# The last store of a gated attention-and-FFN kernel, cut into two halves by partitions and issued from two queues

## The chip, the cores and the metric

The kernel runs on one core of one Trainium2 chip. Its time is device microseconds for one execution: the median of 3 runs is 281.86 us (281.77 to 281.93). One further execution was taken with the hardware profiler; it took 281.68 us.

## What is computed

A sequence of 2048 tokens of width 640 goes through two branches, and a gate per token mixes them. Branch A is linear attention with 32 heads of width 20, whose feature map is a pair of softmaxes. Branch B is an FFN with a gated GELU of width 1728. Cut to what matters:

```python
# x: (1, 2048, 640); all bf16
q, k, v = split_heads(x @ wqkv)
phi(t)  = concat([softmax(t @ w_phi), softmax(-(t @ w_phi))])
kv, z   = einsum("bhsf,bhsd->bhfd", phi(k), v), sum_s phi(k)
a       = (phi(q) @ kv / (phi(q) @ z + 1e-6)) @ wo
b       = (gelu(x @ w_gate) * (x @ w_up)) @ w_down
g       = sigmoid((x * gate_w).sum(-1, keepdims=True))
out     = g * a + (1 - g) * b          # (1, 2048, 640)
```

## The kernel before

All tensors live in on-chip memory. The 2048 tokens are 16 tiles of 128 tokens, in 4 blocks of 4 tiles. Three parts follow one another on TensorE: the projections and the attention state (`attention_state`), the up and gate products of the FFN (`gateups` in `ffn`), and the products with `w_down` and `wo`, which close the kernel (`downs`, line 999).

`downs` calls `down_pair` (line 912) for two token tiles at a time. Its matmuls sum, in PSUM, the FFN half (`wd_sb`) and the attention half (`wo_sb`) of one piece of the output; each sum is made of two halves of the array's rows, so a piece of the output has an opening pass and a closing one (lines 963 to 978). When a piece is closed, `evac` (line 940) moves it from PSUM to the tile `outsb`, multiplied by the gate of each token `Gm`: ScalarE with an activation (line 948), or, for the last pair of tiles, ScalarE for one column piece and VectorE for the other (line 946).

For the last pair of tiles (`last`) the pieces are cut finer, so that less is left to do after the last matmul (lines 917 to 919): tile 14 in one store of 640 columns, tile 15 in one of 448 (two pieces of 224) and a last one of 192 (two pieces of 96). Each of these three stores is one DMA of 128 partitions from `outsb` to the output in HBM, issued by SyncE (lines 953 and 954). The last of them, 128 rows of 192 bf16 numbers, is 48 KB, 384 bytes to the row.

The order of all work is written out by hand. A small recording layer, `_Sched`, turns each operation into an instruction on its engine and adds the semaphore waits that its reads and writes need. `op` (line 66) is for compute instructions. `dma` (line 84) is for transfers. Each queue has a number of lanes, one semaphore to a lane, taken in turn: 16 for SyncE's queue (`sp`), 4 for ScalarE's (`act`), 2 for GpSimd's (line 144). A transfer waits, on the engine that issues it, until the last transfer on its lane has landed, and until what it reads is written. ScalarE's queue carries two small loads at the start of the kernel (lines 276 and 279), and nothing after that.

At the end `finish` (line 99) makes SyncE wait for every engine's semaphore and then for the last transfer of each lane of each queue, in the order in which they were issued. These waits close the program: its last instruction is SyncE's wait for the last store.

Of the kernel before, what the change touches and what calls it, by code (L numbers as in the profile page):

```python
# [3 lines left out]
P = 128  # L4
# [103 lines left out]
class _Kernel:  # L108
# [803 lines left out]
    def down_pair(self, t0, banks, last):  # L912

        sc = self.sc
        NFC, KD, D = self.NFC - 1, self.KD, self.D
        hk = t0 // 4
        if last:
            parts = [((t0, 0, 320), (t0, 320, 320)), ((t0 + 1, 0, 224), (t0 + 1, 224, 224)),
                     ((t0 + 1, 448, 96), (t0 + 1, 544, 96))]
        else:  # L920
            parts = [((t0, c, 320), (t0 + 1, c, 320)) for c in (0, 320)]
        nw = len(parts)

        def mm(r, j, h, c, opens, x, n):
            t, w0, w = parts[h][j]
            tt, gs, bk, a = t % 4, t % 8, banks[h][j], 64 * r
            end = x == n - 1
            if c <= NFC:
                lhs, rhs = self.hT(hk, c)[a:a + 64, tt * P:(tt + 1) * P], self.wd_sb[a:a + 64, c, w0:w0 + w]
                rd = [("hT", hk, c), "wd"] if c < NFC else [("hT", hk, 13, r), ("wd13", r)]  # L930
            else:
                k = c - NFC - 1
                lhs, rhs = self.goT[a:a + 64, gs, k, :], self.wo_sb[a:a + 64, k, w0:w0 + w]
                rd = [("goT", gs), "wo"]
            sc.op("pe", lambda e: e.matmul(self.bank(bk, w), lhs, rhs, start=opens and x == 0, stop=end and not opens,  # L935
                                           skip_group_check=True),
                  reads=rd, writes=[("ps", bk)] + ([("turn", bk)] if end else []), signal=end,
                  after=[("turn", bk)] if x == 0 and not opens else ())

        def evac(h):  # L940
            for j in (0, 1):
                t, w0, w = parts[h][j]
                bk, dst, g = banks[h][j], self.outsb[:, t % 4, w0:w0 + w], self.Gm[:, t:t + 1]
                rd, wr = [("ps", bk), "Gm"], [("outsb", t % 4, h, j)]
                if last and j == 1:
                    sc.op("dve", lambda e: e.tensor_scalar(dst, self.bank(bk, w), g, None, op0=ALU.mult), reads=rd, writes=wr)
                else:
                    sc.op("act", lambda e: e.activation(dst, self.bank(bk, w), AF.Copy, scale=g), reads=rd, writes=wr)  # L948
            os_ = t0 % 4
            if last:  # L950
                c1 = w0 + w
                c0 = parts[h][0][1]
                sc.dma("sp", lambda e: e.dma_start(self.out[t * P:(t + 1) * P, c0:c1], self.outsb[:, t % 4, c0:c1]),
                       reads=[("outsb", t % 4, h, j) for j in (0, 1)], writes=[("out", t0, h)])
            elif h == nw - 1:
                if t0 < self.TB:
                    rows = self.out[0:self.BT, :].rearrange("(p j) n -> p j n", j=self.TB)[:, t0:t0 + 2, :]
                else:
                    rows = self.out[t0 * P:(t0 + 2) * P, :].rearrange("(j p) n -> p j n", p=P)
                sc.dma("sp", lambda e: e.dma_start(rows[:, :, :], self.outsb[:, os_:os_ + 2, :]),  # L960
                       reads=[("outsb", os_ + j, k, j) for j in (0, 1) for k in range(nw)], writes=[("out", t0, h)])

        wos = [NFC + 1 + k for k in range(KD)]
        opening = list(range(NFC + 1)) + wos
        for part in (range(NFC + 1), range(NFC + 1, len(opening))):
            for h in range(nw):
                for x in part:
                    for r in (0, 1):
                        mm(r, r, h, opening[x], True, x, len(opening))
                    yield None  # L970
        closing = list(range(NFC)) + wos
        for h in range(nw):
            for x, c in enumerate(closing):
                for r in (0, 1):
                    mm(r, 1 - r, h, c, False, x, len(closing))
                if c == closing[-1]:
                    evac(h)
                yield None
# [104 lines left out]
```

## Time and profile before

| what | value |
|---|---|
| median of 3 runs | 281.86 us (281.77 to 281.93) |
| the profiled execution: its time | 281.68 us |
| its span, first to last instruction | 280.4 us |
| around the span | 1.28 us |
| granted TensorE clock | 1.000 |
| TensorE matmul busy | 276.6 us (99%) |
| VectorE busy | 177.3 us (63%) |
| ScalarE busy | 106.4 us (38%) |
| DMA rate, mean over the span | 86 GB/s |
| transfers on SyncE's queue (q1) | 59296 packets, 23.63 MB |
| transfers on ScalarE's queue (q10) | 666 packets, 0.03 MB |

The span is counted from the first instruction to the end of the last one; the time of an execution has some more around it. "Busy" is the time in which an engine has an instruction in work. The instructions that issue DMAs, and those that wait for semaphores, are not counted as busy. A DMA has an issue, a time on the engine that sends it off, and a landing, when its semaphore is complete; between the two, its packets run on the core's 16 DMA engines, which all queues share.

### The profile page before, as it was taken

To read this page: it belongs to the slowest core of one execution; us is meant where nothing else is said; L and a number is where in the kernel's file an instruction comes from. 1 tells how busy PE (TensorE), PEld (TensorE's weight loads), DVE (VectorE), ACT (ScalarE), POOL (GpSimd) and SP (SyncE) were. 2 spreads that over 40 slices of the span, in tenths; PEclk is the share of its full clock that TensorE was granted. 3 is DMA by queue.
4 is the path that set the end of the run, shared out by engine and by line. 5 is a ranking of instruction groups with operands and counts; after the bars stand their busy time and mean duration, and the time that the engine had idled before them with its cause. 6 is when DMAs were issued, how large, how long until landed. Compare 5 with 4: busy or idle time off the path is not lost.

```text
span 280.4 us, 7063 instructions
## 1 busy us (share of the span) xinstructions
PE 276.6 (99%) x2994; PEld 168.1 (60%) x3006; DVE 177.3 (63%) x342; ACT 106.4 (38%) x205; POOL 14.4 (5%) x69
## 2 busy tenths in 40 slices
PE   8999999999999999999999999999999999999997
PEld 4576766666765444444444444445777777777785
DVE  2666999999998524233242234878884883883801
ACT  3347877878783423222323223122112112112021
POOL 7411001101000000000000000000000000000000
DMA  7999069887899910000000000101133142232221
GB/s 217 224 220 189 6 136 165 171 163 146 162 191 273 347 41 0 2 0 0 1 2 0 0 0 2 23 2 26 26 50 108 35 76 56 62 59 66 71 75 47
DMA packets 59994, 24.11 MB, mean 86 GB/s; under 512 B 50874, under 2 KB 59450, under 8 KB 59962
## 3 DMA queue, kind: packets, MB, share of 16 engines
q1 hardware_dynamic: 59296, 23.63, 37.7%
q8 instruction: 23, 0.38, 0.6%
q10 hardware_dynamic: 666, 0.03, 0.2%
q14 instruction: 9, 0.07, 0.1%
HBM read 9.04 MB, written 2.62 MB: 42 GB/s over the span
## 4 chain that ended last, share of the span: by engine, by line
PE 97%; DMA 1%; issue 0%; SPq 0%; ACT 0%
PE ps L466 52%; PE ps L935 29%; PE ps L832 6%; PE ps L610 4%; PE ps L480 2%; PE ps L875 2%; PE ps L646 2%; DMA xtok<-in_A_x_dram 1%; PE ps L406 1%; PE ps L342 0%; SPq L230 0%; ACT outsb L948 0%; PE ps L371 0%
## 5 line engine op out<-in xcount | busy, mean ns | idle before, releaser
L809 ACT ACTIVATE gl<-ps 128x512 bf16<-128x512 f32 x52 | 31.1, 597 | 71.2 <-PE ps L466 56.3
L466 PE MATMUL ps<-xT,wu_sb 128*128 128x512 bf16 x214 | 52.9, 379 | 0.3
L466 PE MATMUL ps<-xT,wg_sb 128*128 128x512 bf16 x214 | 52.7, 379 | 0.3
L466 PE MATMUL ps<-w,xT 128*128 128x368 bf16 (+6 forms) x340 | 51.6, 303 | 0.0
L813 DVE TENSOR_TENSOR hT<-ps,gl 128x512 bf16<-128x512 f32 x34 | 23.4, 691 | 44.5 <-PE ps L466 44.5
L935 PE MATMUL ps<-wd_sb,hT 64*128 64x320 bf16 x648 | 48.2, 296 | 0.0
L948 ACT ACTIVATE outsb<-ps,Gm 128x320 bf16<-128x320 f32 (+2 forms) x31 | 14.6, 516 | 70.3 <-PE ps L935 70.3
L466 PEld LDWEIGHTS ps<-w,xT 128*128 128x128 bf16 x340 | 32.1, 98 | 14.6
L935 PEld LDWEIGHTS ps<-wd_sb,hT 64*128 64x128 bf16 x648 | 30.9, 94 | 11.8
L466 PEld LDWEIGHTS ps<-xT,wu_sb 128*128 128x128 bf16 x220 | 21.5, 98 | 25.6
L466 PEld LDWEIGHTS ps<-xT,wg_sb 128*128 128x128 bf16 x220 | 21.2, 98 | 25.2 <-issue 0.2
L935 PE MATMUL ps<-wo_sb,goT 64*128 64x320 bf16 (+2 forms) x340 | 26.5, 288 | 0.0
L628 DVE TENSOR_REDUCE Dk<-Ek 128x66 f32<-128x1320 bf16 x16 | 24.3, 1520 | 2.3 <-ACT gcol L539 2.3
L637 DVE TENSOR_TENSOR Ek<-Ek,Dk 128x1320 bf16<-128x1320 bf16 x16 | 24.5, 1533 | 0.5
L904 DVE TENSOR_TENSOR O<-ps,RH 128x640 bf16<-128x640 f32 x32 | 24.8, 815 | 0.0
L549 ACT ACTIVATE Ek<-ps 128x627 bf16<-128x627 f32 x32 | 20.5, 693 | 6.0 <-PE ps L610 4.5
L549 ACT ACTIVATE Eqt<-ps 128x627 bf16<-128x627 f32 x32 | 20.6, 704 | 2.4 <-PE ps L466 2.4
L935 PEld LDWEIGHTS ps<-wo_sb,goT 64*128 64x128 bf16 x340 | 15.8, 94 | 5.5
L832 PE MATMUL ps<-xT,wg_sb 64*128 64x512 bf16 x80 | 17.6, 376 | 0.0
L832 PE MATMUL ps<-xT,wu_sb 64*128 64x512 bf16 x80 | 17.6, 376 | 0.0
L935 PE MATMUL ps<-wd_sb,xT 64*128 64x320 bf16 (+2 forms) x270 | 16.0, 269 | 0.0
L893 DVE RECIPROCAL RH<-ps 128x32 f32<-128x32 f32 x16 | 5.7, 356 | 13.4 <-PE ps L875 13.4
(97 smaller groups left out, 222.3 us busy)
## 6 DMA issues: line engine op xcount, KB each, us to landing
out_dram<-outsb SPq DMA_DIRECT2D x7, 320.0 KB, 2.9
wd_sb<-in_B_w_down_dram SPq DMA_DIRECT2D x1, 2080.0 KB, 12.2
wg_sb<-in_B_w_gate_dram SPq DMA_DIRECT2D x5, 224.0 KB, 3.1
wg_sb<-in_B_w_gate_dram SPq DMA_DIRECT2D x5, 192.0 KB, 3.0
wu_sb<-in_B_w_up_dram SPq DMA_DIRECT2D x5, 192.0 KB, 3.9
wo_sb<-in_A_wo_dram SPq DMA_DIRECT2D x1, 800.0 KB, 10.2
xtok<-in_A_x_dram SPq DMA_DIRECT2D x2, 320.0 KB, 3.2
w<-in_A_wqkv_dram SPq DMA_DIRECT2D x4, 160.0 KB, 3.6
```

The lines of the kernel that those rows point to most:

```text
L466: self.sc.op("pe", lambda e: e.matmul(self.ps[:, bank * 512 + c0:bank * 512 + c0 + n], lhs, rhs, start=first, stop=fin), reads=reads, writ ...
L549: self.sc.op("act", lambda e: e.activation(dst, src, AF.Exp, scale=scale), reads=[("ps", b), ("ps", b + 1)], writes=[(name, sl, s)])
L610: self.sc.op("pe", lambda e: e.matmul(out, self.xT[:, kt, t * P:(t + 1) * P], self.w3[:, kt, c:c + 2 * n].rearrange("p (r w) -> p r w", w= ...
L628: self.sc.op("dve", lambda e: e.tensor_reduce(self.Dk[:, se, 0, :].rearrange("p (u h) -> p u h", h=self.HG), self.k_view(se), AX.X, ALU.ad ...
L637: sc.op("dve", lambda e: e.tensor_tensor(v, v, R.rearrange("p (u h) -> p u h", h=self.HG).unsqueeze(3).to_broadcast([P, 2 * self.G, self.H ...
L809: self.sc.op("act", lambda e: e.activation(self.gl[:, slot, :], self.bank(bank), AF.Gelu_apprx_tanh), reads=[("ps", bank)], writes=[("gl", ...
L813: self.sc.op("dve", lambda e: e.tensor_tensor(self.hT(b, c), up, self.gl[:, slot, :], ALU.mult), reads=[upk, ("gl", slot)], writes=[("hT", ...
L832: sc.op("pe", lambda e: e.matmul(self.bank(bk), w[a:a + 64, kt, c * P:(c + 1) * P], self.xT[a:a + 64, kt, b * self.BT:(b + 1) * self.BT], ...
L893: dve(lambda e: e.reciprocal(R(0), Dn[1]), rb, [key(0)], guard=old)
L904: dve(lambda e, o=o, f=f, s=s: e.tensor_tensor(o, V[s][:, :, 0:DH], f, ALU.mult), rb[2 * s:2 * s + 2] + [key(6 + s)], [("O", s, sl)], guar ...
L935: sc.op("pe", lambda e: e.matmul(self.bank(bk, w), lhs, rhs, start=opens and x == 0, stop=end and not opens, skip_group_check=True), reads ...
L948: sc.op("act", lambda e: e.activation(dst, self.bank(bk, w), AF.Copy, scale=g), reads=rd, writes=wr)
```

## The change

The last of the three closing stores (`h == nw - 1`, the 48 KB one) becomes two. Partitions 0 to 63 go from SyncE's queue and partitions 64 to 127 from ScalarE's. Each half is 64 rows of 192 numbers, 24 KB. Both read both column pieces of `outsb`, so both wait for VectorE's and for ScalarE's last evacuation. The other two stores, of 640 and 448 columns, stay whole and stay on SyncE's queue. The key that each store writes in the recording layer gets the first partition as a fourth part, so the second half does not wait for the first.

```diff
             if last:
                 c1 = w0 + w
                 c0 = parts[h][0][1]
-                sc.dma("sp", lambda e: e.dma_start(self.out[t * P:(t + 1) * P, c0:c1], self.outsb[:, t % 4, c0:c1]),
-                       reads=[("outsb", t % 4, h, j) for j in (0, 1)], writes=[("out", t0, h)])
+                for q, a, n in (("sp", 0, 64), ("act", 64, 64)) if h == nw - 1 else (("sp", 0, P),):
+                    sc.dma(q, lambda e: e.dma_start(self.out[t * P + a:t * P + a + n, c0:c1],
+                                                    self.outsb[a:a + n, t % 4, c0:c1]),
+                           reads=[("outsb", t % 4, h, j) for j in (0, 1)], writes=[("out", t0, h, a)])
```

## The prediction, made before the changed kernel ran

> **What bounds the kernel now.** I read the page's busy times and chain first, then the timeline of the last microseconds, then the DMA issues of that stretch, then its DMA activity in stretches cut at the first and last packets. The page's fourth part:
>
> ```profile
> PE 276.6 (99%) x2994; PEld 168.1 (60%) x3006; DVE 177.3 (63%) x342; ACT 106.4 (38%) x205; POOL 14.4 (5%) x69
> ...
> PE 97%; DMA 1%; issue 0%; SPq 0%; ACT 0%
> ```
>
> TensorE sets 97% of the time, and the change touches none of its instructions. What it can move is only what comes after the last matmul. The timeline from 278 us on (start, duration, engine, line):
>
> ```profile
> 278.04 0.38 PE L935 MATMUL ps<-wo_sb,goT 64*128 64x96 bf16 x10
> 278.45 0.32 DVE L946 TENSOR_SCALAR outsb<-ps,Gm 128x96 bf16<-128x96 f32 x1 [0.31 <-PE ps L935]
> 278.49 0.34 ACT L948 ACTIVATE outsb<-ps,Gm 128x96 bf16<-128x96 f32 x1 [0.32 <-PE ps L935]
> ```
>
> The matmuls end at 278.42. VectorE and ScalarE evacuate side by side and end at 278.77 and 278.83. Then only the store is left. The line's own view and the DMA view give its issue and landing, and the stretches show where its packets lie (columns: stretch, length, five engines' busy time, clock, DMA share, GB/s):
>
> ```profile
> L953 SPq DMA_DIRECT2D out_dram<-outsb x3: 332/344/345, 276.6 to 278.9; - x3
> ...
> out_dram<-outsb SPq DMA_DIRECT2D x1, 160.0 KB, 1.8
> out_dram<-outsb SPq DMA_DIRECT2D x1, 112.0 KB, 1.7
> out_dram<-outsb SPq DMA_DIRECT2D x1, 48.0 KB, 1.5
> ...
> 279.06:279.52 0.46, 0.00 (x0) 0.00 (x0) 0.00 (x0) 0.00 (x0) 0.00 (x0) 1.00 0.73 249
> 279.52:279.68 0.16, 0.00 (x0) 0.00 (x0) 0.00 (x0) 0.00 (x0) 0.00 (x0) 1.00 0.00 0
> 279.68:279.84 0.16, 0.00 (x0) 0.00 (x0) 0.00 (x0) 0.00 (x0) 0.00 (x0) 1.00 0.75 211
> 279.84:279.99 0.15, 0.00 (x0) 0.00 (x0) 0.00 (x0) 0.00 (x0) 0.00 (x0) 1.00 0.42 103
> 279.99:280.40 0.41, 0.00 (x0) 0.00 (x0) 0.00 (x0) 0.00 (x0) 0.00 (x0) 1.00 0.00 0
> ```
>
> The three issues take 0.332 to 0.345 us whatever their size. The 448-column store's packets are gone by 279.52, so the last store runs alone. Its single records in the trace are finer than these stretches: issue from 278.854 to 279.186, first packet 279.688, last completion packet ending 279.990, SyncE's wait for it recorded from 280.371 to 280.399, which ends the span. So the tail of 1.545 us from issue to end is 0.834 to the first packet, 0.302 with packets running, 0.381 from the last packet to the wait, and 0.028 for the wait. Only the 0.302 has to do with how much is stored.
>
> **The change part by part.** In the built program VectorE, TensorE and GpSimd have the same rows of instructions as before. SyncE's last store has 64 rows instead of 128, ScalarE has one more DMA behind its last activation, and SyncE one more closing wait.
>
> SyncE's half. Starting the transfer hardly depends on its rows: the 960-line store at 269.37 has 256 row pieces, takes 0.372 to issue and 0.888 to its first packet; the store at 276.60 has 128 and takes 0.345 and 0.845. That is 0.043 us for 128 pieces, so 64 pieces fewer are worth about 0.02: first packet at about 278.854 + 0.834 - 0.02 = 279.67.
>
> ScalarE's half. Nothing is queued behind this DMA on ScalarE, and nobody waits for that engine afterwards but SyncE's closing waits. Its queue has 4 lanes and used two, so there is no wait for a lane. It waits for VectorE (done 278.77) and for ScalarE's own last evacuation (278.83). SyncE's issue began 0.025 after that same end, so I take the same start, 278.85 to 278.87. The price that the trace does not show is how long ScalarE's queue takes to its first packet on a quiet chip. The only rows are at the start:
>
> ```profile
> 2.86 0.44 ACTq L276 DMA_DIRECT2D wphi_sb<-in_A_w_phi_dram  x1
> 3.33 0.67 ACTq L279 DMA_DIRECT2D gz<-in_gate_w_dram  x1
> ...
> 2.86:3.75 0.89, 0.89 (x5) 0.41 (x3) 0.00 (x0) 0.00 (x0) 0.64 (x5) 1.00 1.03 392
> ```
>
> The first was issued at 2.856 and its first packet came at 4.619: 1.763 us. That is the upper bound. But it had 640 row pieces, and the 16 DMA engines were full (share 1.03) with SyncE's loads; SyncE's own loads of that time waited as well: the 96 KB piece issued at 2.194 (its 768-byte packets are told apart by their size) shows none before 3.75, over 1.5 us. Issue itself was 0.442 on ScalarE against 0.432 on SyncE around it, 0.010 apart. The lower bound is SyncE's row less the rows saved, 0.81. At the end of the kernel the engines are empty and the shape is a plain row store, so the quiet row is the nearer one: I take 0.834 + 0.010 - 0.02 = 0.82, first packet at about 278.86 + 0.82 = 279.68. Against the value taken the upper bound costs 1.763 - 0.82 = 0.94.
>
> Packets. Both halves come out at about the same moment, 0.01 apart. The 128 data packets of about 0.022 us each are the same and run on the same 16 engines: 8 to an engine before, 4 + 4 now, with one more completion packet (0.009). Bounded below, half of the 0.302 would go (-0.15), if the spread of starts over the engines, not the engines themselves, made that time; bounded above, nothing goes and the extra completion packet adds 0.01. 8 packets at 0.022 are 0.18 of the 0.302 by themselves, and they stay, so I take 0.
>
> The Trainium skill speaks against the change here: "DMA: Bandwidth & Descriptors", section "Rules for kernel authors", says of two transfers to disjoint partition halves not to bother, because both halves spray over all 16 engines, from one queue or from two, and serialize. By that rule the packet term is 0; were the halves truly parallel, the term would be -0.15. No run here yet shows which.
>
> Closing waits. The closing waits that find their semaphore already full follow each other every 0.06 us in the records (279.232, 279.296, 279.357 and so on). One more is added behind the wait for SyncE's half. If ScalarE's half has landed by then it costs 0.06; if it lands later, the wait itself is the end and the 0.06 is hidden. I take half, +0.03.
>
> The sum: -0.02 (rows) + 0.01 (ScalarE's issue) + 0.01 (0.006 and less of later start) + 0 (packets) + 0.01 (completion packet) + 0.03 (closing wait) = +0.04 us. Against the profiled execution: span 280.40 + 0.04 = 280.44, with 1.28 around it 281.72. The median of the runs shown lies 0.18 above the profiled time (281.86 - 281.68), so the forecast is 281.9. If the whole size-dependent part had gone, 0.302, it would still be only 0.1% of the time.
>
> **The rivals.** Within 0.2% means within 0.56 us of 281.86; that is about what a measurement of this kernel can tell from no change.
>
> *Two halves in parallel.* Each queue generates half of the rows, and the packets need only half of 0.302. Then -0.15 - 0.02 = -0.17, and 281.69. For it: the packets' starts spread over 0.27 us, more than the 0.18 that one engine's packets need. Against it: the DMA share of 0.75 in the first half of that time says that the engines were mostly occupied. It is not faster by 0.2% even so.
>
> *One generator, one after the other.* ScalarE's half is prepared only after SyncE's issue is through, 0.33 later. The packets of that half then start at 280.00 instead of 279.67 and take half of 0.302: the end moves by 0.33 - 0.15 = +0.18, to 282.04. For it: the late first packet at 4.619. Against it: in 2.67 to 3.62 the two queues' issues overlap and SyncE's stay at 0.432.
>
> *ScalarE's queue is slow to start* (the other side). Its second use in the kernel, 276 us after the first, has the only price that the trace shows for that queue, 1.763 to the first packet. Then that half ends the kernel: +0.94, and 282.8, slower by 0.33%. It decides once ScalarE's first packet comes more than about 0.85 + 0.56 = 1.4 us after its issue. For it: the row; SyncE's first DMA of all, on idle engines, took 1.048 (0.803 to 1.851), 0.2 over its warm rows, so a queue may start cold. Against it: the backlog of that time explains the row, and the cold 0.2 alone gives only 282.1.
>
> *The change does not do what it says.* It could have been that both halves land on one queue or wait for each other. The built order has one 64-row store at the end of each of the two engines, each waiting for VectorE and ScalarE alone. I leave it out.
>
> **How the numbers follow.** The forecast (end moved by between -0.1 and +0.15) gets 0.57, parallel halves 0.15, one generator 0.09, the slow start 0.16; 0.03 is left for something that makes it faster, which no row supports, since three fixed pieces (0.834, 0.381 and 0.028) make up 1.24 of the 1.545 and none is removed. The first three are all within 0.2%: 0.81, of which I move 0.02 to slower for a mix of a cold start and one generator. So faster 0.03, same 0.79, slower 0.18. The range goes from the parallel halves less the spread of the runs (281.69 - 0.09 = 281.6) to the upper bound of ScalarE's start, 282.8.
>
> **What would show it.** In the changed profile: ScalarE's DMA issue at about 278.86 of about 0.34 us; 24 KB stores with landings of about 1.5 us on both queues; packets on q10 beside those on q1 from about 279.68 to 279.99; the last closing wait at about 280.4. A half that lands after 2 us or more, on ScalarE's queue, would show the slow start; packets ending near 279.84, parallel halves; q10 packets that begin when q1's are done, one generator. Wrong would be an end beyond 281.0 in the span, or any change in TensorE's stream ahead of 278.4.

## The result: slower by 0.24%

The changed kernel takes 282.57 us in the median of 13 runs (282.29 to 283.11), the kernel before 281.93 us in the median of 13 runs (281.60 to 282.47). The ratio is 1.0024, with a 95% interval of 1.0016 to 1.0031: slower by 0.64 us. That it is slower is clear of the noise; whether by more than 0.2% is not, since the interval begins at 0.16%.

The changed kernel's profiled execution took 283.11 us with a span of 281.9, which is 1.5 us more than the span before, not 0.6. Most of that comes from the other end of the kernel. Two lines from the chain of waits of the first 20 us, before and after (start, duration, what):

```profile
1.27 3.41 DMA xtok<-in_A_x_dram
...
5.19 4.56 PE ps L480 x36
```

```profile
2.20 4.07 DMA w<-in_A_wqkv_dram
...
6.31 4.31 PE ps L480 x34
```

The loads that open the kernel landed later in the second execution. From the projections on, everything lies 0.88 us later (the first matmul of line 466 at 10.94 and at 11.82, the last evacuation's end at 278.83 and at 279.71), by the same amount from there to the end of the matmuls. The change does not touch that part, and it differs from profile to profile: in the eleven profiles of this document that first matmul begins anywhere from 10.83 to 11.93 us, and the times of the kernel before spread over 0.87 us. What can be compared between single profiles is the tail, from the end of ScalarE's last evacuation to the end of the span. It was 278.829 to 280.399, 1.570 us. Now it is 279.711 to 281.862, 2.151 us: 0.581 more, which is the 0.64 of the medians within their spread.

The profile after has these lines: the two DMA queues of the page; ScalarE's timeline at the end; the three stores of SyncE and the one of ScalarE by their line (issue in ns, min/median/max); landings by size; and stretches cut at the packets (stretch, length, five engines, clock, DMA share, GB/s):

```profile
q1 hardware_dynamic: 59232, 23.61, 38.6%
...
q10 hardware_dynamic: 746, 0.05, 0.2%
```

```profile
279.37 0.34 ACT L948 ACTIVATE outsb<-ps,Gm 128x96 bf16<-128x96 f32 x1 [0.32 <-PE ps L935]
279.74 0.57 ACTq L954 DMA_DIRECT2D out_dram<-outsb  x1
```

```profile
L954 SPq DMA_DIRECT2D out_dram<-outsb x3: 344/344/536, 277.5 to 279.7; - x3
L954 ACTq DMA_DIRECT2D out_dram<-outsb x1: 575/575/575, 279.7 to 279.7; - x1
```

```profile
out_dram<-outsb SPq DMA_DIRECT2D x1, 24.0 KB, 1.8
out_dram<-outsb ACTq DMA_DIRECT2D x1, 24.0 KB, 2.1
```

```profile
280.41:280.93 0.52, 0.00 (x0) 0.00 (x0) 0.00 (x0) 0.00 (x0) 0.00 (x0) 1.00 0.00 0
280.93:281.19 0.26, 0.00 (x0) 0.00 (x0) 0.00 (x0) 0.00 (x0) 0.00 (x0) 1.00 0.36 95
281.19:281.20 0.01, 0.00 (x0) 0.00 (x0) 0.00 (x0) 0.00 (x0) 0.00 (x0) 1.00 0.00 0
281.20:281.47 0.27, 0.00 (x0) 0.00 (x0) 0.00 (x0) 0.00 (x0) 0.00 (x0) 1.00 0.35 91
281.47:281.87 0.40, 0.00 (x0) 0.00 (x0) 0.00 (x0) 0.00 (x0) 0.00 (x0) 1.00 0.00 0
```

The split did what it says: 64 packets left q1, and q10 has 80 more (64 of data, and 16 completion packets of 4 bytes, which raise the transfer's semaphore). The two issues begin together (279.736 and 279.741 in the single records), but they take 0.536 and 0.575 us where the whole store took 0.332. SyncE's other two stores, of 128 rows, still take 0.344. SyncE's packets start 1.195 us after its issue began instead of 0.834. And there are two bursts of packets with a gap between them: q1's from 280.931 to 281.190, then q10's from 281.201. So 24 KB from SyncE land later (1.8 us) than 48 KB did before (1.5).

### The profile page after: what moved, and what is told of

Read it like the earlier page. It is cut to its first block, busy times and chain, and to the rows that moved or that the text cites. A ratio compares the mean times of both kernels' runs of the same rounds, so it can differ in the third digit from the quotient of the medians.

```text
span 281.9 us, 7066 instructions
## 1 busy us (share of the span) xinstructions
PE 276.8 (98%) x2994; PEld 168.1 (60%) x3006; DVE 177.3 (63%) x342; ACT 106.3 (38%) x205; POOL 14.3 (5%) x69
## 4 chain that ended last, share of the span: by engine, by line
PE 97%; DMA 1%; SPq 0%; issue 0%; ACT 0%
PE ps L466 52%; PE ps L935 29%; PE ps L832 6%; PE ps L610 4%; PE ps L480 2%; PE ps L875 2%; PE ps L646 2%; DMA w<-in_A_wqkv_dram 1%; PE ps L406 1%; SPq L230 0%; SPq L251 0%; ACT outsb L948 0%; PE ps L371 0%
```

## The experiments

Three causes were possible for the slow start: the two issues disturb each other, ScalarE's queue is slow, or a store of 64 rows is slow by its shape. Each kernel is read by its tail, from one profiled execution each. The same kind of store repeats well between them: the four first stores of 64 rows on SyncE take 0.536 to 0.540 us to issue and 1.195 to 1.201 to the first packet. Where medians are given, they are over several runs and the ratio is to the kernel before in the same session; e1, e4, e8 and e9 have a single execution. In the table, the first packet counts from the beginning of its issue; SP is SyncE, ACT is ScalarE. The flag of the rows from e6 on is explained after e4.

| kernel | issue, us | first packet, us | tail, us |
|---|---|---|---|
| before: 128 rows on SP | 0.332 | 0.834 | 1.570 |
| changed: 64 on SP, 64 on ACT | 0.536, 0.575 | 1.195, 1.460 | 2.151 |
| e1: 64 on SP alone | 0.539 | 1.196 | 1.882 |
| e2: 64 and 64 on SP | 0.540, 0.587 | 1.196, 1.248 | 2.519 |
| e3: 128 on ACT | 0.377 | 0.884 | 1.630 |
| e4: 64 on SP, 64 on ACT 0.42 later | 0.540, 0.543 | 1.201, 1.198 | 2.297 |
| e5: 48 on SP, 80 on ACT | 0.346, 0.382 | 0.850, 0.906 | 1.690 |
| e6: 128 on SP, no flag | 0.560 | 1.216 | 1.954 |
| e7: columns, 128 rows each | 0.332, 0.372 | 0.828, 0.871 | 1.705 |
| e8: 48 and 80, no flag | 0.606, 0.622 | 1.261, 1.536 | 2.238 |
| e9: 48 with flag, 80 without | 0.344, 0.614 | 0.842, 1.274 | 1.978 |

**e1, SyncE's half alone.**

```diff
-                for q, a, n in (("sp", 0, 64), ("act", 64, 64)) if h == nw - 1 else (("sp", 0, P),):
+                for q, a, n in (("sp", 0, 64),) if h == nw - 1 else (("sp", 0, P),):
```

> Only SyncE's half of the last store is left; rows 64 to 127 of the last 192 columns are not stored. The tail (end of the last evacuation to end of span) was 1.57 us before and 2.15 after. If the two issues disturb each other because they begin together (one shared generator), this half alone has an issue of 0.31 to 0.34 us, its first packet 0.81 to 0.84 after the issue began, and a tail of 1.45 to 1.55. If a store of 64 rows is slow by its shape, the issue is about 0.54, the first packet comes at about 1.20, and the tail is 1.75 to 1.85.

The three stores of SyncE by their line, and the last one's landing:

```profile
L954 SPq DMA_DIRECT2D out_dram<-outsb x3: 344/345/539, 277.0 to 279.2; - x3
...
out_dram<-outsb SPq DMA_DIRECT2D x1, 24.0 KB, 1.8
```

With ScalarE's queue silent the issue takes 0.539 us, the same as beside it, and the first packet comes as late. So half of the store, alone, has a tail 0.312 longer (1.882 - 1.570) than the whole store had, a little more than the shape was expected to cost. That the two issues disturb each other does not explain SyncE's half. My theory of the collision fell here.

**e2, both halves on SyncE.**

```diff
-                for q, a, n in (("sp", 0, 64), ("act", 64, 64)) if h == nw - 1 else (("sp", 0, P),):
+                for q, a, n in (("sp", 0, 64), ("sp", 64, 64)) if h == nw - 1 else (("sp", 0, P),):
```

> Both halves are issued by SyncE, one behind the other. If the collision of the two engines' issues is what costs, neither issue is stretched: two of 0.32 to 0.34 us, first packets at 0.82 and at 0.82 + 0.36 = 1.18 after the first issue began, tail 1.57 - 0.15 + 0.36 = 1.75 to 1.85, so 0.2 to 0.3 us slower than before and 0.3 faster than the changed kernel. If the shape is slow, two issues of 0.54 and a tail of 2.2 or more. If ScalarE's queue alone was slow, the tail is near that of before, 1.6 to 1.8.

All stores of SyncE by their line:

```profile
L954 SPq DMA_DIRECT2D out_dram<-outsb x4: 344/442/587, 276.6 to 279.5; - x4
```

Two issues of 0.540 and 0.587 and a tail of 2.519; 283.06 us in the median, ratio 1.0035 (1.0023 to 1.0047). This is what the shape predicts. The second queue of the changed kernel thus did save something against two halves on one queue: 2.519 - 2.151 = 0.368 us, less than one issue. The Trainium skill's "DMA: Bandwidth & Descriptors", section "Issuing engines are not separate DMA queues", says that starting DMAs from several engines only saves the time in which a sequencer initiates them; these two tails agree.

**e3, the whole store on ScalarE.**

```diff
-                for q, a, n in (("sp", 0, 64), ("act", 64, 64)) if h == nw - 1 else (("sp", 0, P),):
+                for q, a, n in (("act", 0, P),) if h == nw - 1 else (("sp", 0, P),):
```

> The whole last store, 128 rows, is issued by ScalarE alone. If the cost is the collision, ScalarE's queue behaves as SyncE's: issue 0.33 to 0.36 us, first packet at 0.83 to 0.87, tail 1.55 to 1.62, time within 0.05 us of the kernel before. If ScalarE's queue starts slowly (1.46 us to the first packet in the changed kernel), the issue is about 0.5 to 0.6, the first packet comes at 1.2 to 1.5, and the tail is 1.95 to 2.2.

ScalarE's issue in its timeline, and the landing:

```profile
279.22 0.38 ACTq L954 DMA_DIRECT2D out_dram<-outsb  x1
```

```profile
out_dram<-outsb ACTq DMA_DIRECT2D x1, 48.0 KB, 1.6
```

First packet at 0.884, tail 1.630; 281.92 us in the median, ratio 1.0000 (0.9991 to 1.0009). ScalarE's queue, used for the first time since the start of the kernel, costs 0.05 to 0.06 us against SyncE's. The rival of a queue that starts slowly falls.

**e4, ScalarE's half later.** ScalarE repeats an evacuation of 128x224 into a tile that nobody reads, ahead of its DMA.

```diff
+                if h == nw - 1:
+                    for src, d_ in ((self.bank(banks[h][0], 224), self.Og[:, 0, 0:224]),):
+                        sc.op("act", lambda e: e.activation(d_, src, AF.Copy, scale=g),
+                              reads=[("ps", banks[h][0]), "Gm"], writes=[("Og", 0)])
...
-                           reads=[("outsb", t % 4, h, j) for j in (0, 1)], writes=[("out", t0, h, a)])
+                           reads=[("outsb", t % 4, h, j) for j in (0, 1)] + ([("Og", 0)] if q == "act" else []), writes=[("out", t0, h, a)])
```

> As the changed kernel, but ScalarE first repeats an evacuation of 128x224 into a tile that nobody reads, so that its DMA issue begins some 0.35 us after SyncE's. If the two issues disturb each other only while they overlap, SyncE's issue is back at 0.32 to 0.34 us with its first packet at 0.82, ScalarE's takes 0.33 to 0.36 with its first packet at 0.82 to 0.86 of its own start, and the tail is 0.35 + 1.45 = 1.8 to 1.9: shorter than the 2.15 of the changed kernel although one half starts later. If ScalarE's queue is slow by itself, its first packet comes 1.2 to 1.46 after its issue and the tail is 2.2 to 2.5.

Both queues' stores by their line:

```profile
L958 SPq DMA_DIRECT2D out_dram<-outsb x3: 344/345/540, 276.8 to 279.1; - x3
L958 ACTq DMA_DIRECT2D out_dram<-outsb x1: 543/543/543, 279.5 to 279.5; - x1
```

Neither reading explains it. SyncE's issue stays at 0.540, so the collision is not it; and ScalarE's half of 64 rows comes to its first packet in 1.198, just as SyncE's does. That and the tail of 2.297 are about what was expected of a slow queue, but e3 shows that the queue is not slow. What the two engines share is the shape. One more reading: issued 0.42 us apart, ScalarE's half does not have the extra 0.26 (1.460 - 1.198) that it had in the changed kernel.

**What is special about 64 rows.** In the built programs, the stores of 128 rows and those of 64 differ in one thing besides the number of rows. Each store of 128 rows carries a flag, `ant_dge_precooked`, set by the program's builder from the shape; the stores of 64 rows do not. Of stores built with 16, 32, 48, 64, 80, 96, 100, 112, 120, 127 and 128 rows only the one of 64 lacks it; of these, 48, 64, 80 and 128 were run. The next kernels separate flag from rows.

**e5, 48 rows and 80, both with the flag.**

```diff
-                for q, a, n in (("sp", 0, 64), ("act", 64, 64)) if h == nw - 1 else (("sp", 0, P),):
+                for q, a, n in (("sp", 0, 48), ("act", 48, 80)) if h == nw - 1 else (("sp", 0, P),):
```

> The last store is cut after partition 48 instead of 64: 48 rows on SyncE, 80 on ScalarE. In the built program every store of 128 rows carries a flag, ant_dge_precooked, that the stores of 64 rows lack; those of 48 and 80 rows carry it. If the flag decides, the issues are 0.33 to 0.38 us although they begin together, SyncE's first packet comes 0.82 to 0.85 after its issue began, ScalarE's 0.88 to 1.10, the tail is 1.57 to 1.70 and the time is within 0.15 us of the kernel before. If a store with fewer rows than 128 is slow, issues of about 0.54, first packets at 1.2 and later, and a tail of 2.1 to 2.2 as in the changed kernel.

The line's view and the landings:

```profile
L954 SPq DMA_DIRECT2D out_dram<-outsb x3: 344/344/346, 277.0 to 279.3; - x3
L954 ACTq DMA_DIRECT2D out_dram<-outsb x1: 382/382/382, 279.3 to 279.3; - x1
...
out_dram<-outsb ACTq DMA_DIRECT2D x1, 30.0 KB, 1.6
out_dram<-outsb SPq DMA_DIRECT2D x1, 18.0 KB, 1.4
```

The slow issue is gone, beside another queue and with fewer rows than 128. The tail is 1.690. The median of 282.22 us is 0.30 above that of before, twice the 0.15 that was expected at most; its ratio, 1.0008 (0.9998 to 1.0018), does not tell it from no change, and the tail's +0.120 (0.04%) lies inside it.

**e6, the kernel before, whole store, without the flag.**

```diff
+                self.nc.dge_precook = h < nw - 1
                 sc.dma("sp", lambda e: e.dma_start(self.out[t * P:(t + 1) * P, c0:c1], self.outsb[:, t % 4, c0:c1]),
                        reads=[("outsb", t % 4, h, j) for j in (0, 1)], writes=[("out", t0, h)])
+                self.nc.dge_precook = True
```

> The kernel before, whole store of 128 rows on SyncE, but built without the flag on this one store. If the flag decides, the issue takes 0.53 to 0.60 us, the first packet comes 1.18 to 1.22 after the issue began, and the tail is 1.57 + 0.36 = 1.90 to 1.97; time 0.36 us above the kernel before. If the number of rows decides, nothing changes: issue 0.33, first packet 0.83, tail 1.57.

The three stores by their line, and the last one's landing:

```profile
L954 SPq DMA_DIRECT2D out_dram<-outsb x3: 345/345/560, 277.6 to 279.8; - x3
...
out_dram<-outsb SPq DMA_DIRECT2D x1, 48.0 KB, 1.9
```

The same 128 rows on the same queue, without the flag: issue 0.560 instead of 0.332, first packet 1.216 instead of 0.834, tail 1.954, that is 0.384 more. The median of 282.26 us has a ratio of 1.0013 (1.0004 to 1.0022); 0.384 is 0.14%. The program differs from the one before in nothing else. So the flag decides, not the rows.

**e7, halves by columns.** Each engine stores the 96 columns whose evacuation it waits for, ScalarE its own, SyncE VectorE's.

```diff
-                sc.dma("sp", lambda e: e.dma_start(self.out[t * P:(t + 1) * P, c0:c1], self.outsb[:, t % 4, c0:c1]),
-                       reads=[("outsb", t % 4, h, j) for j in (0, 1)], writes=[("out", t0, h)])
+                for q, a, z, js in (("act", c0, w0, (0,)), ("sp", w0, c1, (1,))) if h == nw - 1 else (("sp", c0, c1, (0, 1)),):
+                    sc.dma(q, lambda e: e.dma_start(self.out[t * P:(t + 1) * P, a:z], self.outsb[:, t % 4, a:z]),
+                           reads=[("outsb", t % 4, h, j) for j in js], writes=[("out", t0, h, a)])
```

> The last store cut by columns: ScalarE stores the 96 columns that it evacuated, SyncE the 96 that VectorE evacuated, each 128 rows with the flag, each after its own evacuation only. If the flag decides, issues of 0.33 to 0.38 us, first packets 0.83 to 0.90 after each issue began unless the second queue's packets wait for the first's (then ScalarE's 1.0 to 1.15), tail 1.57 to 1.75, time within 0.2 us of the kernel before. If two queues at once are what is slow, both issues stretch to 0.5 or more and the tail is 2.0 or more.

The stores by their line, and the last ones' landings:

```profile
L954 SPq DMA_DIRECT2D out_dram<-outsb x3: 332/344/344, 276.7 to 278.9; - x3
L954 ACTq DMA_DIRECT2D out_dram<-outsb x1: 372/372/372, 279.0 to 279.0; - x1
...
out_dram<-outsb SPq DMA_DIRECT2D x1, 24.0 KB, 1.4
out_dram<-outsb ACTq DMA_DIRECT2D x1, 24.0 KB, 1.6
```

Both halves start like whole stores, SyncE's 0.05 us earlier than before since VectorE is done first, and the two queues' packets overlap (279.746 to 280.009 and 279.848 to 280.109). Still the tail is 1.705, 0.135 longer; median 281.96, ratio 1.0000 (0.9991 to 1.0009).

**e8 and e9, the 48/80 split with the flag taken off both or off ScalarE's.** What was left open was why ScalarE's half waited another 0.26 in the changed kernel. The edit of e8, against e5; e9 has `q == "sp"` in place of `h < nw - 1`:

```diff
+                    self.nc.dge_precook = h < nw - 1
                     sc.dma(q, lambda e: e.dma_start(self.out[t * P + a:t * P + a + n, c0:c1],
                                                     self.outsb[a:a + n, t % 4, c0:c1]),
                            reads=[("outsb", t % 4, h, j) for j in (0, 1)], writes=[("out", t0, h, a)])
+                    self.nc.dge_precook = True
```

> Rows 0 to 47 on SyncE, 48 to 127 on ScalarE, both built without the flag. What is asked is why ScalarE's packets began 0.27 us after SyncE's in the changed kernel though both issues began together: if two transfers without the flag are prepared one after the other, SyncE's first packet comes at about 1.20 after its issue, ScalarE's 0.2 or more later, and the tail is 2.05 to 2.2. If that wait has to do with the 64 rows alone, ScalarE's packets begin within 0.1 us of SyncE's and the tail is 1.95 to 2.05.

> The same split, the flag on SyncE's 48 rows, none on ScalarE's 80. If only two transfers without the flag queue behind one another, SyncE's first packet is at 0.83 to 0.85, ScalarE's at 1.20 to 1.26 after its issue began, as alone, and the tail is 1.90 to 2.0. If any two issues that begin together disturb each other's preparation, ScalarE's first packet comes at 1.4 or later and the tail is 2.1 or more.

The stores of e8 by their line, its stretches cut at its packets, and the stores of e9:

```profile
L955 SPq DMA_DIRECT2D out_dram<-outsb x3: 344/344/606, 276.7 to 279.0; - x3
L955 ACTq DMA_DIRECT2D out_dram<-outsb x1: 622/622/622, 279.0 to 279.0; - x1
```

```profile
280.22:280.45 0.23, 0.00 (x0) 0.00 (x0) 0.00 (x0) 0.00 (x0) 0.00 (x0) 1.00 0.33 80
280.45:280.50 0.05, 0.00 (x0) 0.00 (x0) 0.00 (x0) 0.00 (x0) 0.00 (x0) 1.00 0.00 0
280.50:280.79 0.29, 0.00 (x0) 0.00 (x0) 0.00 (x0) 0.00 (x0) 0.00 (x0) 1.00 0.42 106
```

```profile
L955 SPq DMA_DIRECT2D out_dram<-outsb x3: 344/345/345, 277.3 to 279.5; - x3
L955 ACTq DMA_DIRECT2D out_dram<-outsb x1: 614/614/614, 279.5 to 279.5; - x1
```

Without the flag on both, the two bursts with a gap are back although no store has 64 rows, and ScalarE's first packet comes 1.536 after its issue; the tail, 2.238, is a little over the upper end of what was expected. With the flag on SyncE's half alone, ScalarE's comes at 1.274, a little over what was expected too, but far from 1.4 and close to the 1.261 of the 48 rows of e8 without the flag: there is no second wait. (No run has the 80 rows without the flag alone.) So two stores without the flag, issued together from the two queues, have their packets prepared one after the other; one with the flag does not stand in the way of one without. The wait runs from start to start rather than to the end of the first burst: the second burst begins 0.270 after the first in the changed kernel and 0.279 in e8, although the first burst is 64 rows in one and 48 in the other; and in e4, issued 0.42 apart, there is none. What unit does that the trace does not name, and it rests on single executions.

## Why the prediction was wrong, and where it was right

The range, 281.6 to 282.8, held the 282.57, but by luck: its upper end was the price of a slow start of ScalarE's queue, and that queue is not slow (e3). The likeliest case did not happen: the end moved by 0.58 in the tail where +0.04 was forecast, and the median came out 0.24% slower, where "within 0.2%" had 79% and slower 18%. The span ended beyond 281.0, the prediction's own sign of being wrong, though 0.88 of that is the opening. The tail's 0.581 is made of three differences between the two profiles. SyncE's first packet comes 0.361 later (1.195 - 0.834). From it to the last completion packet it now takes 0.536 instead of 0.302, so 0.234 more. From there to the end it takes 0.395 instead of 0.409, so 0.014 less.

- *"Starting the transfer hardly depends on its rows ... 64 pieces fewer are worth about 0.02."* This is the step that failed: +0.361 instead of -0.02. The rows that I drew the line through, of 128 and 256 pieces, all carry the flag, and I continued it past them to a shape that has none. e6 shows the size of it without any change of rows, 0.382 to the first packet (1.216 - 0.834). The built order that I read names shapes but not the flag. The trace of before had the shape: two loads of 64 rows at line 325, two of the three `wd_sb` loads here, in the middle of a row of loads with a steady issue:

```profile
L325 SPq DMA_DIRECT2D wd_sb<-in_B_w_down_dram x3: 441/1014/2458, 86.8 to 89.8; - x3
```

  Their 1.014 and 2.458 us, against the 0.39 to 0.44 of their neighbours, would have been a warning. The DMA engines were 93% busy there, behind a load of 2 MB, so they are no price.

- *Packets, "I take 0".* This failed too: +0.234, since two stores without the flag are prepared one after the other (e8, e9). The rule of the Trainium skill that I set beside it ("DMA: Bandwidth & Descriptors", "Rules for kernel authors": two transfers to disjoint partition halves serialize on the 16 engines that they share, so use one) is right in its advice: no split here gained. But the engines that the halves share are not what kept them apart in the changed kernel: these were 0.36 and 0.35 busy in the two bursts and idle between. In e5, with the flag on both, the bursts do overlap on them (SyncE's from 0.875 to 1.078 after the evacuation, ScalarE's from 0.937 to 1.191), and it still gains nothing. The lower bound, -0.15 for half of the packets, was not to be had either: 64 rows alone (e1) take 0.263 from the first packet to the last completion packet, where the 128 rows of e6, also without the flag, take 0.308 and those of before 0.302.

- *ScalarE's queue.* The value that I took for a plain store on a quiet chip was close: 0.82 was forecast for 64 rows, and e3 measured 0.884 for 128. So the upper bound of 1.763 is not the price of that queue by itself; that the backlog at the start made it, as argued, no run tested.

- *The rivals.* "ScalarE's queue is slow to start" has the right sign, and its half did come after the 1.4 us from which it was to decide (1.460), but for another reason: the same queue without the 64 rows is not slow (e3, e5). "One generator, one after the other" has a true core, the two bursts, but its price was too low, +0.18, because it did not have the slow start. Both rivals' signs came at once: ScalarE's half landed 2.1 us after its issue, and q10's packets began as q1's ended (281.201 and 281.196). So the signs could not tell which it was; the experiments could. Halves that run in parallel and take half the time did not occur in any run.

- *The closing wait, +0.03.* ScalarE's half lands last, so the wait behind SyncE's is hidden and that term is 0 here. e7, where SyncE's half is waited for last and had landed already, shows it: two closing waits at 1.616 and 1.677 after the evacuation, 0.061 apart. Of its 0.135 that is nearly half; the rest is the last increment of the semaphores, 0.075 later than before (1.600 against 1.525).

- *That TensorE's stream ahead of the tail stays as it was* holds: the same 2994 matmuls, and the same time from the beginning of the first matmul of line 466 to the end of the last of line 935 (267.48 us in both profiles).

No version tried here beats the kernel before; the whole store on SyncE's queue, with the flag, has the shortest tail.

## What to carry to other kernels

Splitting a small store at the end of a kernel had next to nothing to win here: its packets are 0.3 of its 1.5 us, and half the rows took off only some 0.04 of that. Two queues bring two sets of completions, and one more wait where that wait comes last: +0.12 to +0.14 us even in the good cases (e5, e7). Before pricing a DMA by another one's row, check that both have the same built form: the flag that 64 rows lack was worth 0.38 us on one store, and cutting at partition 48 instead of 64 kept it. When two single profiles differ by more than the change can explain, compare stretch by stretch; here 0.88 of 1.46 us came from the opening loads.

## What the runs showed of the hardware that was not expected

- The flag makes two kinds of this last store: an issue of 0.33 to 0.38 us with it and of 0.54 to 0.62 without, first packets at 0.83 to 0.91 and at 1.20 to 1.27 where no store without the flag from the other queue stood ahead. (Earlier in the kernel, with other traffic, issues with the flag are longer too: the stores of line 960 take 0.350 to 0.522.) Two without it that begin together on two queues come one after the other, 0.27 to 0.28 us apart (the changed kernel: 281.201 - 280.931; e8: 0.279).
- Each store completes with 16 increments of its semaphore, recorded about 0.011 us apart, so that they take 0.167 us for the one store before (1.358 to 1.525 after the evacuation). With two stores they follow each other: in e5 16 increments from 1.276 to 1.440, then 16 from 1.458 to 1.646. The last completion packet of e5 is only 0.036 us later than before (1.197 against 1.161), but the last increment is 0.121 later, which is the whole difference of the tails (0.120). That the increments queue behind one another is read from these records, and the other profiles fit it: from the last completion packet to the last increment it is 0.449 in e5 and 0.438 in e7, where the two stores' packets end 0.10 to 0.11 apart, but 0.364 before, 0.371 in e3 and 0.361 in e6 with one store, and 0.353 in e9, where the second store's packets end 0.50 after the first's. No run was made to test it.
